# A seventh of w2 taken by a gather in mid-run instead of at the end: GQA decode attention beside a Mish layer, on one core

## The chip, the cores and the metric

One core of one Trainium2 chip. The metric is device time in microseconds of one launch, the median of several runs. Names of the engines: PE multiplies matrices (PEld is its weight load), DVE is the vector engine, ACT the scalar engine, POOL the general one, SP the one that issues most DMAs. Sixteen DMA engines move the bytes.

## What is computed

For 8 sequences, one new token each (D = 512), the result is the sum of three terms: the input, an attention block, and a two-layer block, both of the normalised input.

```python
xn = layernorm(x)                                   # x is 8 x 1 x 512
q  = xn @ wq                                        # 32 heads of 128
s  = q . k_cache * 128**-0.5                        # k_cache, v_cache: 8 x 8 x 8192 x 128
o  = softmax(s) . v_cache                           # four query heads share a KV head
A  = o @ wo                                         # wo is 4096 x 512
h  = xn @ w1 + b1                                   # w1 is 512 x 1792
act = h * tanh(softplus(h))                         # Mish
Bm = act @ w2                                       # w2 is 1792 x 512
out = x + A + Bm
```

All is float32. The two caches are 537 MB of the 561 MB that are read.

## The kernel before, in words

The work is cut into 32 units j = 0 to 31, each a sequence b = j % 8 and a pair of KV heads m = j // 8. A unit reads 8 MB of keys and 8 MB of values, each by one DMA of 128 partitions x 64 KB that SP issues (`load_unit`, L119). All of these land in one large tile `kv`. Its first quarter holds V (`V_AT`). The keys of even units lie at `ROW`, those of odd units half a place later at `ROW + ROW // 2`, so that two key loads overlap by half: the load of the next keys can be issued when the first half of the present scores is done.

The order of instructions is written out by hand; each engine runs its own in the order of the code, and waits are put in where data or places demand it. A unit goes: first half of `scores(j)` on PE (L284), issue of the keys of unit j+1, second half of `scores(j)`, `softmax(j)` (L294: DVE finds the maxima, PE turns them, ACT takes the exponentials), `values(j-1)` on PE (L346), issue of the values of unit j, `key_weights(j+1)` on DVE (L267), then `turn(j)`: PE brings the exponentials into another order by four products with `perm` (L323), a product with `ones` (L324), DVE transposes (L328) and sums (L334), and `merge(j-1)`. In unit 0 there is no `values`, and `mish` stands between `key_weights(1)` and `turn(0)`.

The start, before the loop: load of wq's first quarter into the tile `ws`, load of the keys of unit 0, small constant tiles on POOL and DVE, the layer norm, `xres` (the input in the layout of the result, L204), `selections` (L209), load of w1, `project(0)` (L223 to L242), load of the keys of unit 1, `spread` (L249).

`mish` (L367) multiplies by w1 and b1 on PE (L371, L380), computes the activation on DVE and ACT (L388 to L403) in a stretch of `kv` that begins at `W1_AT = ROW`, then lays it out by two products (L407), transposes it in blocks of 32 (L413) and copies what is needed to `aT` (L414). The keys of unit 2 later land on that same stretch. For the heads of the next quarter, `load_q` reads wq into `ws` in units 4, 12 and 20, and `project` uses it in units 5, 13 and 21.

The end: behind the loop SP issues four loads of wo (2 MB each) and three of w2 (2, 1 and 0.5 MB). PE does `values(31)`, the four steps of `outputs` with wo (L423), `merge`, and the products with w2 (`down`, L435), where a partition holds seven rows of 4 KB of w2. ACT copies wo's sum (L505); it is added to w2's sum by PE (L508) after the first w2 part. DVE adds `xres` (L518), and the result goes out (L519).

Of the kernel before, what the change touches and what calls it, by code (L numbers as in the profile page):

```python
# [20 lines left out]
F = 1792  # L21
# [3 lines left out]
G = 4  # L25
NH = 2
TG = SK // (NH * G) // P
BW = 1024
CC = D // P
FG = F // G  # L30
FT = 4
FP = FG // FT
Q = P // G
# [28 lines left out]
LOAD_Q, MAKE_Q, SPREAD_Q = 4, 5, 7  # L62


@with_exitstack
def kernel(
# [20 lines left out]
    kv = const.tile([P, PLACES], F32, name="kv")  # L87
    ws = const.tile([P, CC * BW], F32, name="ws")
# [4 lines left out]
    M = psum.tile([P, 512], F32, name="m")  # L93
    H = psum.tile([P, 512], F32, name="h")
# [15 lines left out]
    aT = const.tile([P, 2 * W2R, B], F32, name="aT")  # L110
    pt8 = const.tile([P, HALF, PL * TL, H2], F32, name="pt8")
    tr = const.tile([P, PL * TL, 32], F32, name="tr")

    def load_q(m):

        rows = wq.rearrange("j p f -> (j p f)").rearrange("(m p f) -> m p f", m=NP, p=P)
        nc.sync.dma_start(ws, rows[m])

    def load_unit(src, j, at):  # L119
        m, b = divmod(j, B)  # L120
        lo = (b * HKV + 2 * m) * NH * G
        t = kv[:, at : at + ROW]
        nc.sync.dma_start(
            t,
            src[lo : lo + NB].rearrange("j p f -> (j p f)").rearrange("(p f) -> p f", p=P),
        )
        return t


    low = kv[:B, W1_AT : W1_AT + 3 * D]  # L130
# [4 lines left out]
    for r in range(4):  # L135
        n = FG // 8
# [59 lines left out]
    for g in range(G):  # L196
# [170 lines left out]
    def mish(w1_t, b1_sb, flat):  # L367
        hp = H[:, :FG]
        for c in range(CC):
            for g in range(G):  # L370
                nc.tensor.matmul(  # L371
                    hp[Q * g : Q * g + B, :],
                    xnT[:, c, :],
                    w1_t[:, c * 2 + g // 2, g % 2 * FG : (g % 2 + 1) * FG],
                    start=(c == 0),
                    stop=False,
                )
        for g in range(G):
# [24 lines left out]
        nc.vector.tensor_mul(t1, t2, z)  # L403
        act = one
        half = FG // 2
        for e in range(2):
            nc.vector.tensor_mul(  # L407
                act.rearrange("p (i a e l) -> p e a l i", a=2, e=2, i=W2R)[:, e],
                h[:, half * e : half * (e + 1)].rearrange("p (a l i) -> p a l i", a=2, i=W2R),
                t1[:, half * e : half * (e + 1)].rearrange("p (a l i) -> p a l i", a=2, i=W2R),  # L410
            )
        turned = flat[:, 5 * FG : 6 * FG]
        nc.vector.transpose(turned, act)  # L413
        nc.vector.tensor_copy(aT, turned.rearrange("p (j q) -> p j q", q=Q)[:, :, :B])  # L414


    A = X[:, 0]

    def outputs(m, t):
        w = t.rearrange("p (u f) -> p u f", u=4)  # L420
        for d in range(2):
            for h in range(REP):
# [5 lines left out]
                    stop=(m == NP - 1 and d == 1),  # L428
                )

    def down(lo, hi, w):
        for j in range(2 * lo, 2 * hi):
            for g in range(G):
                at = (j - 2 * lo) * D + g * P
                nc.tensor.matmul(  # L435
                    H[Q * g : Q * g + B, :P],
                    aT[:, j, :],
                    w[:, at : at + P],
                    start=(j == 0),
                    stop=(j == 2 * W2R - 1),  # L440
                )


# [7 lines left out]
    for j in range(UNITS):  # L451
        b = j % B
        more = j // B + 1 < NP

        k = k_t.pop(j)
        scores(j, k, j % 2 == 1, 0)
        if j == UNITS - 1:
            v_t[j] = load_unit(v, j, K_AT[0])
        elif j > 0:
            k_t[j + 1] = load_unit(kT, j + 1, K_AT[(j + 1) % 2])  # L460
        scores(j, k, j % 2 == 0, 1)
        WK.pop(j)
        lsel = softmax(j)
        os = None
        if j > 0:
            os = values(j - 1, v_t.pop(j - 1))
        if j + 1 < UNITS:
            v_t[j] = load_unit(v, j, V_AT)
            if more and b == SPREAD_Q:
                spread(qT)  # L470
            key_weights(j + 1)
        if j == 0:
            mish(w1_t, b1_sb, kv[:, W1_AT : W1_AT + 6 * FG])
        if more and b == LOAD_Q:
            load_q(j // B + 1)
        if more and b == MAKE_Q:
# [9 lines left out]
    for m in range(NP):  # L486
# [4 lines left out]
    w2_rows = w2.rearrange("j p f -> (j p) f").rearrange("(q i) f -> q (i f)", i=W2R)  # L491
    w2_t = []
    parts = ((0, 4), (4, 6), (6, 7))
    for lo, hi in parts:
        t = kv[:, W2_AT + lo * BW : W2_AT + hi * BW]
        nc.sync.dma_start(t, w2_rows[:, lo * BW : hi * BW])  # L496
        w2_t.append(t)

    os = values(UNITS - 1, v_t.pop(UNITS - 1))
# [3 lines left out]
    outputs(NP - 1, w_o[NP - 1])  # L503
    a_sb = work.tile([P, 512], F32, name="e")
    nc.scalar.copy(a_sb, A)  # L505
    down(*parts[0], w2_t[0])
    for g in range(G):
        nc.tensor.matmul(  # L508
            H[Q * g : Q * g + B, :P],
            bsel[:, :B],  # L510
            a_sb[:, g * P : (g + 1) * P],
            start=False,
            stop=False,
        )
# [43 lines left out]
```

## Time and profile before

| | |
|---|---|
| median of 3 runs | 1313.15 us (1312.73 to 1313.54) |
| the profiled execution's own time | 1312.88 us |
| its span, first to last instruction | 1311.1 us |
| granted TensorE clock, mean | 0.872 |
| PE busy | 995.4 us (76%) |
| DVE busy | 515.6 us (39%) |
| ACT, POOL busy | 40.2 us, 4.4 us |
| DMA | 561.79 MB, 428 GB/s over the span |

The page cuts the span in 40 slices and gives each engine's share; it also follows back the chain of work that ended last. A row of a timeline reads: start in us, duration in us, engine, line, operation, out<-in, shapes, how many, and in brackets the engine's idle time before it and what ended that. A `q` behind an engine's name (SPq) means its instruction queue; a DMA row there is the issue, not the transfer. A row of busy times in a stretch reads: from:to, length, then busy time and count of PE, PEld, DVE, ACT and POOL (those that were asked for), granted clock, DMA share and GB/s. A float32 product shows as two matmuls on PE, so four products are eight.

### The profile page before, as it was taken

How to read it: one execution, taken by the hardware profiler on the slowest of the kernel's cores; microseconds unless marked ns; L12 is line 12 of the kernel's file. 1: busy time of each engine (PE TensorE's matmuls, PEld its weight loads, DVE VectorE, ACT ScalarE, POOL GpSimd, SP SyncE). 2: the span in 40 equal slices, each digit the busy share in tenths (PEclk: the TensorE clock that was granted, in tenths of full speed). 3: DMA queues.
4: the chain of work that ended last, by engine and by line, in shares of the span. 5: the costliest groups of instructions: out<-in, count | busy, mean ns of one | idle time of the engine just before them, and what ended most of it. 6: DMA issues, size and time to landing. Idle time of an engine off the chain costs nothing.

```text
span 1311.1 us, 11174 instructions
## 1 busy us (share of the span) xinstructions
PE 995.4 (76%) x5048; PEld 341.6 (26%) x5048; DVE 515.6 (39%) x728; ACT 40.2 (3%) x88; POOL 4.4 (0%) x13
## 2 busy tenths in 40 slices
PE   5978777778868768887878768687796678677766
PEld 3322222223322222232322222232232222222222
DVE  2373344432444442345342444413544433344431
ACT  1000000000000000000000000000000000000000
POOL 1000000000000000000000000000000000000000
PEclk9988878898887899778987888888888899787898
DMA  9999999999999999999999999999999999999998
GB/s 393 450 420 440 428 436 428 431 440 428 437 428 436 428 439 424 443 424 438 426 435 438 423 440 422 442 426 434 436 431 434 432 432 432 430 431 432 425 415 326
DMA packets 13711, 561.79 MB, mean 428 GB/s; under 512 B 1368, under 2 KB 1496, under 8 KB 4704
## 3 DMA queue, kind: packets, MB, share of 16 engines
q1 hardware_dynamic: 13520, 561.06, 99.3%
q8 instruction: 39, 0.64, 0.2%
q10 hardware_dynamic: 16, 0.02, 0.0%
q14 instruction: 8, 0.07, 0.0%
q0 software_dynamic: 128, 0.01, 0.0%
HBM read 561.01 MB, written 0.07 MB: 428 GB/s over the span
## 4 chain that ended last, share of the span: by engine, by line
DMA 72%; PE 23%; DVE 2%; SPq 2%; issue 0%; ACT 0%; POOL 0%; POOLq 0%; DVEq 0%
DMA kv<-in_v 70%; PE o L346 20%; DMA kv<-in_w 2%; SPq L496 2%; PE s L284 1%; DVE pt L334 1%; PE x L249 1%; PE m L234 0%; PE h L223 0%; PE h L371 0%; DVE kv L402 0%; DVE tr L328 0%; DVE wk L267 0%; POOL kv L137 0%; DVE nm L296 0%
## 5 line engine op out<-in xcount | busy, mean ns | idle before, releaser
L284 PE MATMUL s<-kv,wk 128*64 128x512 f32 x2048 | 509.7, 661 | 171.2 <-DMA kv<-in_kT 168.6
L346 PE MATMUL o<-kv,pt 128*32 128x512 f32 x2048 | 267.9, 683 | 49.1 <-DMA kv<-in_v 39.6
L284 PEld LDWEIGHTS s<-kv,wk 128*64 128x64 f32 x2048 | 157.0, 153 | 498.5 <-issue 324.5
L334 DVE TENSOR_REDUCE pt<-tr 64x512 f32<-64x2048 f32 x64 | 241.3, 3770 | 1.6
L296 DVE TENSOR_REDUCE nm<-s 128x1 f32<-128x512 f32 x32 | 22.1, 692 | 368.7 <-PE s L284 368.7
L323 PE MATMUL x<-e,perm 128*128 128x512 f32 x256 | 130.8, 658 | 2.0 <-ACT qr L256 2.0
L346 PEld LDWEIGHTS o<-kv,pt 128*32 128x32 f32 x2048 | 69.3, 123 | 221.3 <-issue 169.5
L354 DVE TENSOR_SCALAR os<-o,isel 128x128 f32<-128x128 f32 x32 | 11.2, 351 | 268.5 <-PE o L346 268.5
L328 DVE STREAM_TRANSPOSE tr<-x 128x512 f32<-128x512 f32 x128 | 78.7, 672 | 0.0
L323 PEld LDWEIGHTS x<-e,perm 128*128 128x128 f32 x256 | 50.8, 209 | 76.9 <-issue 74.5
L267 DVE TENSOR_TENSOR wk<-qr,mask 128x512 f32<-128x512 f32 x64 | 63.0, 1026 | 19.8 <-ACT qr L256 19.8
L315 ACT ACTIVATE e<-s,nmx 128x512 f32<-128x512 f32 x32 | 22.0, 687 | 1097.9 <-DVE nmx L312 1097.9
L356 DVE SCALAR_TENSOR_TENSOR os<-o,isel,os 128x128 f32<-128x128 f32 x96 | 33.7, 351 | 3.4
L297 PE MATMUL m<-ident,nm 128*1 128x128 f32 x32 | 8.7, 273 | 30.1 <-DVE nm L296 30.1
L308 PE MATMUL m<-ident,nx 1*128 1x1 f32 x32 | 7.0, 219 | 24.2 <-DVE nx L304 24.2
L326 DVE RECIPROCAL rt<-m 128x8 f32<-128x8 f32 x32 | 6.6, 207 | 38.5 <-PE m L324 38.5
L249 PE MATMUL x<-qT,tr 128*128 128x64 f32 x128 | 19.3, 315 | 3.0 <-ACT qr L256 2.7
L249 PEld LDWEIGHTS x<-qT,tr 128*128 128x128 f32 x128 | 18.1, 226 | 6.2 <-ACT qr L256 3.3
L363 PE MATMUL m<-hsel,os 128*128 128x8 f32 x64 | 12.4, 266 | 9.3 <-DVE rt L326 9.3
L317 DVE TENSOR_SCALAR lsel<-rsel,l 128x8 f32<-128x8 f32 x32 | 7.4, 231 | 30.1 <-ACT e L315 30.1
L297 PEld LDWEIGHTS m<-ident,nm 128*1 128x1 f32 x32 | 2.5, 79 | 58.3 <-DVE nm L296 58.3
L324 PEld LDWEIGHTS m<-lsel,ones 128*128 128x128 f32 x64 | 12.2, 190 | 15.8 <-issue 15.5
(89 smaller groups left out, 165.3 us busy)
## 6 DMA issues: line engine op xcount, KB each, us to landing
ws<-in_wq SPq DMA_DIRECT2D x4, 2048.0 KB, 34.3
kv<-in_wo SPq DMA_DIRECT2D x4, 2048.0 KB, 25.8
kv<-in_w SPq DMA_DIRECT2D x1, 3584.0 KB, 22.7
kv<-in_w SPq DMA_DIRECT2D x1, 2048.0 KB, 37.1
kv<-in_w SPq DMA_DIRECT2D x1, 1024.0 KB, 20.7
kv<-in_kT SPq DMA_DIRECT2D x32, 29.9
kv<-in_v SPq DMA_DIRECT2D x32, 29.9
kv<-in_w SPq DMA_DIRECT2D x1, 512.0 KB, 20.7
```

Of the source, the lines that this page charges most:

```text
L249: nc.tensor.matmul(X[:, half, k * 64 : (k + 1) * 64], wide[:, half * 8 + k], qT, start=True, stop=True,)
L267: nc.vector.tensor_mul(w[:, :, d], q[:, :, d].to_broadcast([P, DI, NH * G, REP]), mask[:, d * NH * G : (d + 1) * NH * G] .rearrange("p (o ...
L284: nc.tensor.matmul(S[64 * c : 64 * (c + 1), :], w[:, i].rearrange("p d k h -> p (d k h)"), kk[:, i, c, :], start=(part == 0 and n == 0), s ...
L296: nc.vector.tensor_reduce(nm, S, axis=AX.X, op=ALU.max, negate=True)
L315: nc.scalar.activation(e, S, AF.Exp, bias=nmx, accum_out=l)
L323: nc.tensor.matmul(X[:, g], perm[:, g], e, start=True, stop=True)
L328: nc.vector.transpose(tr.rearrange("p (l t) c -> p t l c", t=TL)[:, tl], X.rearrange("p g (t q l) -> p t l g q", t=TL, q=PP)[:, tl],)
L334: nc.vector.tensor_reduce(pt8[half, :, :, d * REP : (d + 1) * REP].rearrange("p c y h -> p y c h"), tr[half].rearrange("p y (g c h) -> p y ...
L346: nc.tensor.matmul(O[Q * q : Q * (q + 1), :], pt8[:, c, TL * l : TL * (l + 1), :].rearrange("p t h -> p (t h)"), vt[:, 512 * n : 512 * (n ...
L356: nc.vector.scalar_tensor_tensor(os, O[:, DH * i : DH * (i + 1)], isel[:, i : i + 1], os, op0=ALU.mult, op1=ALU.add)
L363: nc.tensor.matmul(M[:, 168 : 168 + H2], os, hsel, start=True, stop=True)
L496: nc.sync.dma_start(t, w2_rows[:, lo * BW : hi * BW])
```

## The change

A partition keeps six instead of seven rows of 4 KB of w2 for the end (written as twelve half rows of 2 KB, `FU`). The remaining 128 rows, half a MB, are read in unit 14 by an indirect DMA from POOL into `ws`, on 64 of the 128 partitions, 8 KB each (`load_extra`), and multiplied in unit 17 (`extra`), whose result is added to `xres`. Which partition takes which row stands in `RUNS`; the indices are built in the start by `find_rows` (POOL writes them as a row, DVE picks each partition's own). A second index tile, from `MARKS`, drives a gather of 36 rows of 256 B of wq in unit 26, whose data nobody reads. In `mish` the layout of the activation changes, the part that belongs to the gathered rows is put into `ex` by 20 small copies, and PE turns it into `eT`. At the end w2 comes in five transfers (1 MB, 768, 512, 512 and 256 KB), and wo's sum is added ahead of all w2 products instead of after the first part.

```diff
-W2R = 7
+W2R = 6
+FU = 2 * W2R
+FE = 4
+NONE = 65536
+MARKS = tuple(
+    (p0, p0, n)
+    for p0, n in ((0, 1), (4, 2), (8, 3), (16, 4), (28, 4), (60, 1), (64, 4), (96, 2))
+    + ((68, 4), (100, 3), (92, 4), (124, 4))
+)
+RUNS = (
+    ((0, 12), (16, 4)),
+    ((28, 4), (32, 12)),
+    ((48, 4), (60, 4), (64, 8)),
+    ((92, 4), (96, 8), (124, 4)),
+)
...
+LOAD_E, USE_E = 14, 17
...
+    def find_rows(idx, runs, flat):
+        table = flat[:, :P].bitcast(mybir.dt.int32)
+        real, mine = flat[:, P : 2 * P], flat[:, 2 * P : 2 * P + 1]
+        nc.gpsimd.memset(table, NONE)
+        for at, p0, n in runs:
+            nc.gpsimd.iota(table[:, p0 : p0 + n], pattern=[[1, n]], base=at, channel_multiplier=0)
+        nc.vector.tensor_copy(real, table)
+        nc.vector.tensor_mul(real, real, ident)
+        nc.vector.reduce_sum(mine, real, axis=AX.X)
+        nc.vector.tensor_copy(idx, mine)
...
     nc.vector.tensor_copy(xres, M[:, 256:384])
+    runs = []
+    for g in range(G):
+        at = FG // 4 * g + Q * W2R // 2
+        for p0, n in RUNS[g]:
+            runs.append((at, p0, n))
+            at += n
+    find_rows(idx, runs, kv[:, W1_AT + 7424 : W1_AT + 7424 + 2 * P + 1])
+    find_rows(idm, MARKS, kv[:, W1_AT + 7808 : W1_AT + 7808 + 2 * P + 1])
...
         act = one
-        half = FG // 2
-        for e in range(2):
-            nc.vector.tensor_mul(
-                act.rearrange("p (i a e l) -> p e a l i", a=2, e=2, i=W2R)[:, e],
-                h[:, half * e : half * (e + 1)].rearrange("p (a l i) -> p a l i", a=2, i=W2R),
-                t1[:, half * e : half * (e + 1)].rearrange("p (a l i) -> p a l i", a=2, i=W2R),
-            )
-        turned = flat[:, 5 * FG : 6 * FG]
-        nc.vector.transpose(turned, act)
+        nc.vector.tensor_mul(
+            act.rearrange("p (c e f) -> p e c f", c=2, e=2),
+            h.rearrange("p (e c f) -> p e c f", c=2, e=2),
+            t1.rearrange("p (e c f) -> p e c f", c=2, e=2),
+        )
+        rows = act.rearrange("p (c r) -> p c r", c=2)
+        mixed = flat[:, 5 * FG : 5 * FG + FU * Q]
+        turned = flat[:, 6 * FG : 6 * FG + FU * Q]
+        ex = flat[:, 7 * FG :].rearrange("p (t q) -> p t q", t=FE)
+        for c in range(2):
+            nc.vector.tensor_copy(
+                mixed.rearrange("p (i c l) -> p c l i", i=W2R, c=2)[:, c],
+                rows[:, c, : Q * W2R].rearrange("p (l i) -> p l i", i=W2R),
+            )
+        nc.vector.transpose(turned, mixed)
         nc.vector.tensor_copy(aT, turned.rearrange("p (j q) -> p j q", q=Q)[:, :, :B])
+        nc.vector.memset(ex, 0.0)
+        for g in range(G):
+            at = Q * W2R
+            for p0, n in RUNS[g]:
+                for c in range(2):
+                    nc.vector.tensor_copy(
+                        ex[Q * g : Q * (g + 1), c::2, p0 : p0 + n],
+                        rows[Q * g : Q * (g + 1), c, at : at + 2 * n].rearrange(
+                            "p (s i) -> p i s", i=2
+                        ),
+                    )
+                at += 2 * n
+        for t in range(FE):
+            nc.tensor.matmul(
+                M[:, 384 + t * B : 384 + (t + 1) * B], ex[:, t, :], bsel[:, :B], start=True, stop=True
+            )
+        nc.vector.tensor_copy(eT.rearrange("p t b -> p (t b)"), M[:, 384 : 384 + FE * B])
...
+    def load_extra():
+        nc.gpsimd.indirect_dma_start(
+            ws[:, : FE * D],
+            None,
+            w2.rearrange("j p f -> (j p f)").rearrange("(r f) -> r f", f=FE * D),
+            bass.IndirectOffsetOnAxis(ap=idx, axis=0),
+            bounds_check=F // FE - 1,
+            oob_is_err=False,
+        )
+
+    def extra():
+        for t in range(FE):
+            nc.tensor.matmul(
+                H[Q * t : Q * t + B, :], eT[:, t, :], ws[:, t * D : (t + 1) * D], start=True, stop=True,
+            )
+        part = work.tile([P, 512], F32, name="e")
+        nc.scalar.copy(part, H)
+        for g in range(G):
+            nc.tensor.matmul(
+                M[Q * g : Q * g + B, 256:384], bsel[:, :B], part[:, g * P : (g + 1) * P], start=True, stop=True,
+            )
+        nc.vector.tensor_add(xres, xres, M[:, 256:384])
...
+        if j == 26:
+            nc.gpsimd.indirect_dma_start(
+                ws[:, :64],
...
+        if j == LOAD_E:
+            load_extra()
+        if j == USE_E:
+            extra()
         if more and b == MAKE_Q:
             qT = project(j // B + 1)
         turn(j, lsel)
...
-    parts = ((0, 4), (4, 6), (6, 7))
+    parts = ((0, 4), (4, 7), (7, 9), (9, 11), (11, 12))
     for lo, hi in parts:
-        t = kv[:, W2_AT + lo * BW : W2_AT + hi * BW]
-        nc.sync.dma_start(t, w2_rows[:, lo * BW : hi * BW])
+        t = kv[:, W2_AT + lo * D : W2_AT + hi * D]
+        nc.sync.dma_start(t, w2_rows[:, :, lo * D : hi * D])
...
     nc.scalar.copy(a_sb, A)
-    down(*parts[0], w2_t[0])
     for g in range(G):
         nc.tensor.matmul(
             H[Q * g : Q * g + B, :P],
             bsel[:, :B],
             a_sb[:, g * P : (g + 1) * P],
-            start=False,
+            start=True,
             stop=False,
         )
-    for p, t in zip(parts[1:], w2_t[1:]):
+    for p, t in zip(parts, w2_t):
         down(*p, t)
```

More of the change, by code (lines that the diff above doesn't have):

```diff
@@ L109 @@
     oT = const.tile([P, NP, H2, B], F32, name="oT")
-    aT = const.tile([P, 2 * W2R, B], F32, name="aT")
+    aT = const.tile([P, FU, B], F32, name="aT")
+    eT = const.tile([P, FE, B], F32, name="eT")
+    idm = const.tile([P, 1], mybir.dt.uint32, name="idm")
+    idx = const.tile([P, 1], mybir.dt.uint32, name="idx")
     pt8 = const.tile([P, HALF, PL * TL, H2], F32, name="pt8")
@@ L429, in outputs @@
                 )
+    def load_extra():
[10 more added lines that the diff above has]
+            nc.tensor.matmul(
+                H[Q * t : Q * t + B, :],
+                eT[:, t, :],
+                ws[:, t * D : (t + 1) * D],
+                start=True,
+                stop=True,
+            )
[3 more added lines that the diff above has]
+            nc.tensor.matmul(
+                M[Q * g : Q * g + B, 256:384],
+                bsel[:, :B],
+                part[:, g * P : (g + 1) * P],
+                start=True,
+                stop=True,
+            )
+        nc.vector.tensor_add(xres, xres, M[:, 256:384])
     def down(lo, hi, w):
-        for j in range(2 * lo, 2 * hi):
+        for j in range(lo, hi):
             for g in range(G):
-                at = (j - 2 * lo) * D + g * P
+                at = (j - lo) * D + g * P
                 nc.tensor.matmul(
@@ L438, in down @@
                     w[:, at : at + P],
-                    start=(j == 0),
-                    stop=(j == 2 * W2R - 1),
+                    start=False,
+                    stop=(j == FU - 1),
                 )
@@ L472 @@
         if j == 0:
-            mish(w1_t, b1_sb, kv[:, W1_AT : W1_AT + 6 * FG])
+            mish(w1_t, b1_sb, kv[:, W1_AT : W1_AT + 7 * FG + FE * P])
         if more and b == LOAD_Q:
             load_q(j // B + 1)
+        if j == 26:
+            nc.gpsimd.indirect_dma_start(
+                ws[:, :64],
+                None,
+                wq.rearrange("j p f -> (j p f)").rearrange("(r f) -> r f", f=64),
+                bass.IndirectOffsetOnAxis(ap=idm, axis=0),
+                bounds_check=NONE // 2 - 1,
+                oob_is_err=False,
+            )
[3 more added lines that the diff above has]
+            extra()
         if more and b == MAKE_Q:
@@ L490 @@
         )
-    w2_rows = w2.rearrange("j p f -> (j p) f").rearrange("(q i) f -> q (i f)", i=W2R)
+    w2_rows = w2.rearrange("j p f -> (j p f)").rearrange("(g r) -> g r", g=G)
+    w2_rows = w2_rows[:, : Q * FU * D].rearrange("g (l f) -> g l f", l=Q)
     w2_t = []
-    parts = ((0, 4), (4, 6), (6, 7))
+    parts = ((0, 4), (4, 7), (7, 9), (9, 11), (11, 12))
     for lo, hi in parts:
-        t = kv[:, W2_AT + lo * BW : W2_AT + hi * BW]
-        nc.sync.dma_start(t, w2_rows[:, lo * BW : hi * BW])
+        t = kv[:, W2_AT + lo * D : W2_AT + hi * D]
+        nc.sync.dma_start(t, w2_rows[:, :, lo * D : hi * D])
         w2_t.append(t)
@@ L511 @@
             a_sb[:, g * P : (g + 1) * P],
-            start=False,
+            start=True,
             stop=False,
         )
-    for p, t in zip(parts[1:], w2_t[1:]):
+    for p, t in zip(parts, w2_t):
         down(*p, t)
```

## The prediction

> **What bounds the kernel now.** I read the page first (busy shares, then the chain), then the waits of the DMA queue, then the start and the end in order of time.
>
> ```profile
> span 1311.1 us, 11174 instructions
> DMA  9999999999999999999999999999999999999998
> DMA 72%; PE 23%; DVE 2%; SPq 2%; issue 0%; ACT 0%; POOL 0%; POOLq 0%; DVEq 0%
> SPq L123 <- PE s L284: 299.6, 31, 22.7
> SPq L123 <- DVE aT L414: 17.6, 1, 17.6
> ```
>
> The DMA line is over nine tenths in 39 of 40 slices, and the chain is DMA for 72%. So the kernel is a stream of bytes, and bytes that only change places cost what they cost before. Two things can move the time: a stretch in which the DMA engines have nothing queued, and the tail behind the last byte. SP issues a K or V load when its place is free, so the slack of each issue is what matters. The last two rows are SP's waits: 31 times a K load waits for PE's score matmuls, and once for `aT` (L414), in the start, where this change adds work. These are the rows of that stretch.
>
> ```profile
> 50.67 0.33 SPq L123 DMA_DIRECT2D kv<-in_v  x1
> 68.85 0.33 SPq L123 DMA_DIRECT2D kv<-in_kT  x1
> ```
>
> ```profile
> 56.61 3.70 PE L323 MATMUL x<-e,perm 128*128 128x512 f32 x8
> 60.37 13.95 PE L284 MATMUL s<-kv,wk 128*64 128x512 f32 x64
> ```
>
> ```profile
> 66.23 0.62 DVE L403 TENSOR_TENSOR kv<-kv 128x448 f32<-128x448 f32 x1
> 66.89 0.96 DVE L407 TENSOR_TENSOR kv<-kv 128x224 f32<-128x224 f32 x2
> 67.88 0.65 DVE L413 STREAM_TRANSPOSE kv<-kv 128x448 f32<-128x448 f32 x1
> 68.56 0.22 DVE L414 COPY aT<-kv 128x112 f32<-128x112 f32 x1
> ```
>
> V of unit 0 is issued at 50.67, K of unit 2 at 68.85 (I call them V0 and K2). PE passes from mish straight to turn(0) at 56.61 and to scores(1) at 60.37, while DVE works on mish until 68.78. K2's place holds mish's scratch and half of K1's, so its issue needs both the end of mish and the first half of scores(1) (half of 13.95, done near 67.4). Today mish ends last. Two DMA answers show how much room K2 has.
>
> ```profile
> DMA packets 24, 0.79 MB, mean 605 GB/s; under 512 B 12, under 2 KB 12, under 8 KB 12
> DMA to landing us min/median/max: 26.0/26.0/26.0
> DMA  0000000000000000000000000000000000024799
> ```
>
> The first is of 73.9 to 75.2 us: the 12 packets under 512 B are the marks with which 12 of the 16 engines close V0, and the other 12 are 64 KB rows of K2 that start at once. The second is V0's own landing: 50.67 + 26.0 = 76.67, so the last engines are done near 76.2. The third is of 1308.0 to 1309.5, in 40 slices: the output's transfer, issued at 1308.48 (row below) into empty engines, has its first packets in slice 35, at 1309.3. An issue needs some 0.85 us to its first packet. K2 at 68.85 is thus 74.8 - 0.85 - 68.85 = 5.1 us early for most engines, 6.5 for the last.
>
> **The change part by part.** (a) *mish gets a PE step in its middle.* After the activation DVE makes one product instead of two halves, two copies, the transpose of 384 columns, the copy to `aT`, a memset of 512 columns and 20 small copies into `ex`; then PE multiplies `ex` four times by `bsel`, and DVE copies the result to `eT`. Everything stands inside mish, in front of turn(0). PE takes its instructions in the order of the code, so turn(0), scores(1) and all behind them wait for the last small copy. That is the wait which the change adds, and queued behind it are turn(0) and scores(1) on PE, the transposes and sums of turn(0) on DVE (they wait for PE), and K2 on SP. The prices:
>
> ```profile
> 1.47 0.48 DVE L149 MEMSET o<- 128x512 f32 x1
> 4.66 0.99 DVE L155 COPY perm<-ident 128x16 f32<-128x16 f32 x8 [2.17 <-POOL perm L146]
> 14.44 1.89 DVE L209 COPY tr<-ident 128x2048 f32<-128x2048 f32 x1
> 16.70 1.88 PE L234 MATMUL m<-bsel,e 128*128 128x8 f32 x8 [0.70 <-ACT e L231]
> 244.64 5.18 PE L323 MATMUL x<-e,perm 128*128 128x512 f32 x8
> 562.59 6.63 PE L323 MATMUL x<-e,perm 128*128 128x512 f32 x8
> 1201.07 16.79 PE L284 MATMUL s<-kv,wk 128*64 128x512 f32 x64 [6.14 <-DMA kv<-in_kT]
> 1211.04 0.33 SPq L123 DMA_DIRECT2D kv<-in_kT  x1
> ```
>
> DVE from 66.89: product 0.62 (as L403); two copies of 192 columns, each L414's 0.22 plus 80 columns at 1.89/2048, 0.29, so 0.58; transpose 0.65 x 384/448 = 0.56; `aT` 0.22; memset 0.48; 20 copies at 0.99/8 = 0.12, 2.4. Sum 4.9: `ex` is ready at 71.8. The small copies are the uncertain part: at L414's 0.22 they are 4.4 and `ex` comes at 73.8; if they run together a little, 71.4.
>
> PE then does the four products: L234 does just such four (eight passes) in 1.88, so 73.7. Turn(0) took 3.70 at 56.61; it took 5.18 and 6.63 where PE came out of a stretch with little work. Here PE has been idle since 56.6, for 15 us, so I take 5.2 and keep 3.70 and 6.63 as ends: scores(1) starts at 73.7 + 5.2 + 0.06 = 79.0. Its first half is 7.0, or 1211.04 - 1201.07 = 9.97 after a wait; I take 7.0, since turn(0) has gone before. K2 is issued at 86.0 instead of 68.85.
>
> The granted clock shows what the 5.2 stands for:
>
> ```profile
> 561.70:568.50 6.80, 6.80 (x13) 3.39 (x13) 0.22 (x1) 0.00 (x0) 0.00 (x0) 0.50 0.91 388
> ```
>
> In this window, which holds nearly all of the 6.63 us turn, PE ran at 0.50 for 6.8 us though it was busy throughout. The Trainium skill ("TensorE: Matmul & The Clock Gate", "Part 1: The HAM clock gate") says that PE falls to half clock after an idle window of about 3.4 us and is released after about 3.4 us of sustained work. By that rule only 1.5 us of turn(0) would run slow, it would take about 4.5, and the sum below would be 0.7 smaller (an estimate from the Trainium skill's figure); the trace shows a slow stretch twice as long.
>
> The first bytes of K2 then come at 86.0 + 0.85 = 86.9. Twelve engines were empty around 74.8, the others by 76.2: idle for 12.1 and 10.7 us. I take **12.0**, since most engines have the long gap. Ends: all fast, 71.4 + 1.0 (the four products at half of what they cost there; an estimate) + 3.70 + 0.06 + 7.0 = 83.2, idle 7.9 on the last engines; all slow, 73.8 + 1.9 + 6.63 + 0.06 + 9.97 = 92.4, idle 18.4. No later stage gives this back, as the DMA line has no slack elsewhere.
>
> What is late next: scores(1) ends at 79.0 + 13.95 = 93.0, DVE has turn(0)'s transposes and sums done by then (79.0 + 2.46 + 7.55, rows below). In unit 30 the next V is issued 1229.25 - 1217.86 = 11.4 us after the scores' end (1201.07 + 16.79), so V1 comes at 104.4, first bytes 105.3. K2 leaves the engines at 86.9 + 19.35 = 106.2 (one load is half of the 38.7 us between the two V issues below). That holds by 0.9 us; if PE stays slow, a gap of a microsecond or two more is possible here, and it lies within the ends. From there the rhythm is the old one.
>
> ```profile
> 68.81 2.46 DVE L328 STREAM_TRANSPOSE tr<-x 128x512 f32<-128x512 f32 x4
> 71.37 7.55 DVE L334 TENSOR_REDUCE pt<-tr 64x512 f32<-64x2048 f32 x2
> 1190.55 0.33 SPq L123 DMA_DIRECT2D kv<-in_v  x1
> 1229.25 20.24 SPq L123 DMA_DIRECT2D kv<-in_v  x2
> ```
>
> (b) *Building the indices* (24 POOL instructions, 8 on DVE, before the selections). POOL is free at 5.5 (first row below). DVE, which starts the selections at 14.44 now, first does its eight, 1.8 at L414's 0.22, then the selections' 1.89: done at 18.1. The spread that reads them can't start before qT, 23.02 + 0.23. Cover 5.1 us: zero. If that cover goes, each microsecond counts fully (second rival).
>
> ```profile
> 4.57 0.94 POOL L147 MEMSET pt<- 128x1024 f32 x1
> 23.02 0.23 DVE L242 TENSOR_SCALAR qT<-m 128x64 f32<-128x64 f32 x1 [6.69 <-PE m L234]
> 728.69 1.12 PE L284 MATMUL s<-kv,wk 128*64 128x512 f32 x2 [4.90 <-DMA kv<-in_kT]
> ```
>
> (c) *The gather in unit 14 and extra() in unit 17.* Queued on POOL, which has nothing else then; it waits for the projection's reads of `ws` in unit 13. extra() adds on PE eight passes of 512 columns (3.57/16 each by L423 below, 1.8), ACT's copy (0.58 by L505) and eight passes like L508 (0.40): 2.9 us with the joints, ahead of turn(17). PE then waits 4.90 us for K18 anyway (third row above), so it is hidden. SP's next load of `ws` is three units later. The index gather of unit 26 moves 36 rows of 256 B into a tile that nobody reads: zero.
>
> (d) *The end.* SP issues five transfers where it issued three, 3 MB for 3.5 MB.
>
> ```profile
> 1266.66 21.33 SPq L496 DMA_DIRECT2D kv<-in_w  x3
> 1298.98 3.57 PE L423 MATMUL x<-kv,oT 128*8 128x512 f32 x16 [2.98 <-DMA kv<-in_wo]
> 1302.67 0.58 ACT L505 COPY e<-x 128x512 f32<-128x512 f32 x1 [43.58 <-PE x L423]
> 1303.77 1.93 PE L435 MATMUL h<-kv,aT 128*8 128x128 f32 x64 [1.22 <-DMA kv<-in_w]
> 1305.52 0.40 PE L508 MATMUL h<-e,bsel 128*8 128x128 f32 x8
> 1307.47 0.62 PE L435 MATMUL h<-kv,aT 128*8 128x128 f32 x16 [0.17 <-DMA kv<-in_w]
> 1302.60:1304.60 2.00, 0.83 (x32) 0.83 (x36) 0.00 (x0) 0.58 (x1) 0.00 (x0) 1.00 0.58 242
> 1308.48 0.35 SPq L519 DMA_DIRECT2D out<-os  x1
> ```
>
> SP has its last w2 issue out at 1288.0; two more, even at 5 us each, are out well before the output at 1308.48: zero. In the old time frame PE gets wo's sum at 1303.25, adds it in 0.40, and has 48 products of w2 left (96 passes at 1.93/64 = 0.03, 2.9, and 0.2 for the joints): 1306.8, where it ended at 1308.1. The row of 1302.60 says why this may hold: in those 2 us the DMA share is 0.58, so some seven of 16 engines are already done, and the others set the end. If the gathered half MB rides on engines that are ahead, the lagging ones lose 32 KB each, 1.2 us at 512 KB in 19.35, and the tail gains 1.3. If it rides on all 16, the old bytes are only earlier, and 0.3 is left from the shorter last transfer. If it rides on the lagging ones, 64 KB more and 32 KB less, it costs 1.1. No row tells which; I take **-0.8**, nearer to the first, between it and the second.
>
> The Trainium skill ("DMA: Bandwidth & Descriptors", "The descriptor swizzle") gives each engine fixed groups of four partitions; by it the 64 partitions chosen belong to just eight engines, eight rows each. Whether these are the ones that are ahead it doesn't say; if they are, the tail term is -1.3.
>
> **Sum.** 12.0 - 0.8 = +11.2 us on the profiled execution's 1312.88 (span 1311.1): 1324.1. The median shown is 1313.15, so this is +0.8%; a change of 0.2%, 2.6 us, is about what a measurement of this kernel can tell from none.
>
> **The rivals.** *No gap, no change.* PE would have to run turn(0) and scores(1) ahead of the four products. Then scores(1) ends at 74.3 as now, the products at 76.2, and K2 is issued between 74 and 76.2: idle 0 to 2.3, less 0.8, **1313**. It decides from K2's issue before 74.0. For it: PE does run ahead of DVE at 56.61. Against it: only because nothing in front of turn(0) waits there; every row of PE stands in the code's order.
>
> *POOL holds the start.* DVE's work after POOL's last is 0.9 and the selections 1.89, so POOL must end by 20.5; if it needs over 0.62 us for each of 24 instructions, the selections, the spread and all of unit 0 move. At 0.94, its longest compute row, it ends at 28.1, 7.6 late: **1332**. Against it: the memset behind that row writes 1024 columns, these one to 128. The Trainium skill ("GPSIMD Engine Reference", "2.1 Instruction dispatch") adds some 6 us for the first call of a function freshly loaded; by that the limit falls to 0.37 each. No row here shows such a call.
>
> *The gather lands on lagging engines*, +1.1 in place of -0.8: **1326**. It doesn't hide the gap, it adds to it.
>
> **How the numbers follow.** Forecast 0.83, no gap 0.08, POOL 0.05, gather 0.04. Predicted 1324.1. The ends of all sums are 1312.88 + 7.9 - 1.3 = 1319.5 and 1312.88 + 18.4 + 1.1 = 1332.4; the upper needs every price at its worst, so the range is 1319 to 1330, which leaves out the no-gap case, the POOL case and a rest. Forecast, POOL and gather are slower, 0.92, of which I keep 0.02 back for a gap that PE or SP shortens in a way I don't see: slower 0.90. The other 0.10 is the no-gap case: same 0.07 and, with the best tail, faster 0.03.
>
> **What would show it.** Right: K2 issued near 86 instead of 68.85, PE idle some 15 us between L380 and the four products, one slice of the DMA line far below nine early on, V issues 38.7 apart from there, all later marks 11 to 13 us late, and a tail from wo's last landing to the end about 1 us shorter. Wrong: K2 issued before 75; or POOL still busy past 20 us; or a second gap ahead of V1; or the gather's unit longer than its neighbours by more than the 1.2 us of its bytes.

## The result, and the profile after

The changed kernel takes 1345.72 us (1344.48 to 1347.57, 4 runs) against 1313.35 us before: ratio 1.0248, 95% interval 1.0231 to 1.0266, or 32 us. I had forecast 1324.1 with a range to 1330. The profiled execution took 1344.48 us, 31.6 more than that of before. One execution of `before_step` (below) took 3280.78 us and fell in a slow state, so it is left out. Two lines of the page:

```profile
span 1342.5 us, 11256 instructions
DMA  9969999999999999999999999999999999999992
```

The DMA line shows two holes. The third slice has fallen from nine tenths to six: that is the gap at the start which I forecast. The last slice has fallen from eight to two: that one I did not forecast. First the start, by SP's waits and by the instructions of PE, DVE and SP in order of time:

```profile
SPq L141 <- DVE kv L464: 20.2, 1, 20.2
```

```profile
68.72 1.91 DVE L464 COPY kv<-kv 32x24 f32<-32x24 f32 x20
70.61 1.87 PE L472 MATMUL m<-bsel,kv 128*128 128x8 f32 x8 [14.64 <-DVE kv L464]
72.33 5.24 PE L361 MATMUL x<-e,perm 128*128 128x512 f32 x8
77.63 13.95 PE L322 MATMUL s<-kv,wk 128*64 128x512 f32 x64
84.80 0.33 SPq L141 DMA_DIRECT2D kv<-in_kT  x1
100.68 0.33 SPq L141 DMA_DIRECT2D kv<-in_v  x1
```

PE sits idle for 14.64 us until the last of the 20 small copies, then does the four products, turn(0) at a low pace, and scores(1). SP's wait of 20.2 us for the copies (L464) ends with them at 70.63; then K2 waits 14 us more, for the first half of scores(1), and is issued at 84.80 instead of 68.85. How much of the stream this cost is read from the moments at which PE starts on keys or values that it has waited for. First the keys of unit 5, then the keys and values of unit 14 and the keys of unit 15 (the gather runs beside these); before, then after:

```profile
212.71 16.05 PE L284 MATMUL s<-kv,wk 128*64 128x512 f32 x64 [6.32 <-DMA kv<-in_kT]
...
573.30 16.65 PE L284 MATMUL s<-kv,wk 128*64 128x512 f32 x64 [3.28 <-DMA kv<-in_kT]
592.65 8.63 PE L346 MATMUL o<-kv,pt 128*32 128x512 f32 x64 [0.66 <-DMA kv<-in_v]
612.04 16.06 PE L284 MATMUL s<-kv,wk 128*64 128x512 f32 x64 [6.32 <-DMA kv<-in_kT]
...
1293.78 1.90 PE L423 MATMUL x<-kv,oT 128*8 128x512 f32 x16 [0.55 <-DMA kv<-in_wo]
```

```profile
224.52 16.20 PE L322 MATMUL s<-kv,wk 128*64 128x512 f32 x64 [6.15 <-DMA kv<-in_kT]
...
584.90 16.92 PE L322 MATMUL s<-kv,wk 128*64 128x512 f32 x64 [4.69 <-DMA kv<-in_kT]
605.79 9.82 PE L384 MATMUL o<-kv,pt 128*32 128x512 f32 x64 [1.94 <-DMA kv<-in_v]
625.16 15.14 PE L322 MATMUL s<-kv,wk 128*64 128x512 f32 x62 [5.09 <-DMA kv<-in_kT]
...
1306.47 1.90 PE L484 MATMUL x<-kv,oT 128*8 128x512 f32 x16 [0.82 <-DMA kv<-in_wo]
1313.86 3.60 PE L484 MATMUL x<-kv,oT 128*8 128x512 f32 x16 [5.17 <-DMA kv<-in_wo]
1319.00 1.06 PE L527 MATMUL h<-kv,aT 128*8 128x128 f32 x32 [0.40 <-DMA kv<-in_w]
1326.44 1.47 PE L527 MATMUL h<-kv,aT 128*8 128x128 f32 x24 [6.38 <-DMA kv<-in_w]
1331.43 1.04 PE L527 MATMUL h<-kv,aT 128*8 128x128 f32 x16 [3.52 <-DMA kv<-in_w]
1336.61 1.04 PE L527 MATMUL h<-kv,aT 128*8 128x128 f32 x16 [4.14 <-DMA kv<-in_w]
1339.00 0.62 PE L527 MATMUL h<-kv,aT 128*8 128x128 f32 x8 [1.35 <-DMA kv<-in_w]
```

The difference is 11.8 us at unit 5 and 11.6 at unit 14: the gap at the start, and nothing more until there. Across the gather it becomes 13.1, and at the third step of wo it is 12.7 (1306.47 - 1293.78). From that step to the end of the span it took 17.3 us before (1311.1 - 1293.78) and takes 36.0 now: the missing 18.7 us all lie there. The last step of wo starts 7.4 us behind the third where it was 5.2, and then PE waits for one w2 transfer after the other, 6.38, 3.52, 4.14 and 1.35 us. What those transfers do meanwhile, in a stretch in which nothing but w2 moves (the last two columns are the DMA share and GB/s):

```profile
1319.00:1331.00 12.00, 2.53 (x56) 1.52 (x56) 0.00 (x0) 0.00 (x0) 0.00 (x0) 0.60 0.25 105
```

The DMA share is 0.25 with transfers queued. In the trace's records of single packets, four packets of w2 are under way during 93% of this stretch, and hardly ever fewer. So four of sixteen engines work, at 26 GB/s each. The new view of w2, `g (l f) -> g l f`, has the four groups of 448 features as its outermost dimension.

### The profile page after: what moved, and what is told of

Same layout as the page of the kernel before. It is cut to its first block, busy times and chain, and to the rows that moved or that the text cites. A ratio compares the mean times of both kernels' runs of the same rounds, so it can differ in the third digit from the quotient of the medians.

```text
span 1342.5 us, 11256 instructions
## 1 busy us (share of the span) xinstructions
PE 991.3 (74%) x5056; PEld 341.2 (25%) x5056; DVE 519.1 (39%) x760; ACT 40.8 (3%) x89; POOL 8.9 (1%) x39
## 4 chain that ended last, share of the span: by engine, by line
DMA 71%; PE 23%; SPq 3%; DVE 2%; issue 0%; ACT 0%; POOL 0%; POOLq 0%
DMA kv<-in_v 69%; PE o L384 19%; SPq L602 3%; PE s L322 2%; DMA kv<-in_w 2%; PE x L287 1%; PE x L361 0%; PE m L272 0%; PE h L261 0%; PE h L409 0%; DVE kv L440 0%; DVE wk L305 0%; POOL kv L167 0%; PE m L472 0%; DVE kv L464 0%
## 5 line engine op out<-in xcount | busy, mean ns | idle before, releaser
L384 PE MATMUL o<-kv,pt 128*32 128x512 f32 x2048 | 263.9, 674 | 54.1 <-DMA kv<-in_v 44.5
L527 PE MATMUL h<-kv,aT 128*8 128x128 f32 x96 | 5.2, 365 | 15.8 <-DMA kv<-in_w 15.8
```

The source lines that it names most:

```text
L384: nc.tensor.matmul(O[Q * q : Q * (q + 1), :], pt8[:, c, TL * l : TL * (l + 1), :].rearrange("p t h -> p (t h)"), vt[:, 512 * n : 512 * (n ...
```

## The experiments

Two theories stood at the outset for the end: that the view with 4 outermost leaves w2 on four engines (V), or that the order, the number or the sizes of the five transfers are at fault (P). For the start: that the wait of PE and K2 for the products is the whole 12 us (S), or that something else in the early part is.

**The view at the end.** `end16` cuts each transfer into four of 32 partitions:

```diff
-        nc.sync.dma_start(t, w2_rows[:, :, lo * D : hi * D])
+        for g in range(0, G, 1):
+            nc.sync.dma_start(t[Q * g : Q * (g + 1)], w2_rows[g, :, lo * D : hi * D])
```

> The changed kernel with one edit: each of the five w2 transfers is issued as four, one for each group of 32 partitions; pieces, pitch and places stay. Theory A (four engines: the view of w2 has an outermost dimension of 4, and the transfer runs on four of 16 DMA engines): w2's last landing comes about 7 to 8 us behind wo's last instead of 25, DMA share there well over 0.22, and the time falls by 19 to 20 us to about 1326. Theory B (the small pieces at a pitch of 24 KB are slow in themselves): the time stays within 2 us of 1345.7.

Measured: 1332.55 us, ratio 1.0149 (1.0132 to 1.0166); 13 us of the expected 20 came back. In the end of `end16` the DMA share is no longer a quarter:

```profile
1303.00:1327.00 24.00, 14.55 (x166) 4.93 (x158) 1.58 (x5) 0.59 (x1) 0.00 (x0) 0.72 0.81 220
```

So the view mattered, but either it was not all or the cut had a price. `uniform` keeps whole transfers and lets a partition keep the first six of its seven old rows, so that the view has 128 outermost. The seventh rows then lie elsewhere in w2, and two gathers of 4 KB a partition bring them instead of one of 8 KB. The lines that change the view:

```diff
-    w2_rows = w2.rearrange("j p f -> (j p f)").rearrange("(g r) -> g r", g=G)
-    w2_rows = w2_rows[:, : Q * FU * D].rearrange("g (l f) -> g l f", l=Q)
+    w2_rows = w2.rearrange("j p f -> (j p) f").rearrange("(q i) f -> q (i f)", i=W2R + 1)
...
-        nc.sync.dma_start(t, w2_rows[:, :, lo * D : hi * D])
+        nc.sync.dma_start(t, w2_rows[:, lo * D : hi * D])
```

> The changed kernel, but the six rows a partition keeps for the end are the first six of its seven (one pitch for all 128 partitions, so the view of w2 has 128 outermost instead of 4), still five transfers of the same sizes; the seventh rows come by two gathers of 4 KB instead of one of 8 KB, onto the same 64 partitions. Theory V (the view with 4 outermost confines each w2 transfer to four of the sixteen engines, and that is the whole 18.8 us that I missed at the end; cutting the transfers into pieces of 32 partitions gave back only 13 because the pieces have a cost of their own): DMA share at the end near 1.0 and w2's last landing about 5 to 6 us behind wo's last one minus overlap, as before; the time falls by 20 to 1325 (1323 to 1327), my original sum. Rival P (w2 at the end is slow for another reason: five transfers, the gaps between the rows, or the many issues): the time stays at 1332 or above, as with the cut transfers.

Measured: **1325.03 us** (1324.81 to 1326.24), ratio 1.0094 (1.0078 to 1.0109): 20.7 less than the changed kernel, with the same five transfers in the same order. PE in the end of `uniform`:

```profile
1312.58 2.74 PE L488 MATMUL x<-kv,oT 128*8 128x512 f32 x16 [2.46 <-DMA kv<-in_wo]
1316.04 0.61 PE L617 MATMUL h<-e,bsel 128*8 128x128 f32 x8 [0.73 <-ACT e L615]
1316.43 2.39 PE L532 MATMUL h<-kv,aT 128*8 128x128 f32 x72
1319.31 1.04 PE L532 MATMUL h<-kv,aT 128*8 128x128 f32 x24 [0.50 <-DMA kv<-in_w]
```

The waits of 6.38, 3.52 and 4.14 us are gone; 72 of 96 passes run through, and only 0.50 us is waited for w2. Theory P falls. `before4` turns it round: the kernel before, with nothing but a view of four groups for w2. It moves as many bytes in the same three transfers, but some rows of w2 are left out and others read in their place, so its result is not that of the layer.

```diff
-    w2_rows = w2.rearrange("j p f -> (j p) f").rearrange("(q i) f -> q (i f)", i=W2R)
+    w2_rows = w2.rearrange("j p f -> (j p f)").rearrange("(g r) -> g r", g=G)
+    w2_rows = w2_rows[:, : Q * 6 * BW].rearrange("g (l f) -> g l f", l=Q)
...
-        nc.sync.dma_start(t, w2_rows[:, lo * BW : hi * BW])
+        nc.sync.dma_start(t, w2_rows[:, :, min(lo, 5) * BW : min(hi, 6) * BW])
```

> The kernel before, where only the view of w2 at the end is changed: grouped by four outermost with another pitch inside the group (so wrong rows are read, and the third transfer reads the sixth row again; the same three transfers, the same 3.5 MB, 128 partitions each). No gather, nothing moved. Theory V: w2 runs on four engines; 3.5 MB cost 18.8 x 3.5/3 = 22 more: 1335 (1330 to 1339), DMA share 0.25 in the last 20 us. Rival P (five transfers or their order made the end slow): no change, 1313.

Measured: 1346.46 us (1341.26 to 1347.95), ratio 1.0244 (1.0224 to 1.0264): 33 us from the view alone, where I had expected 22. The size was a miss, and this row of `before4` holds most of it:

```profile
1304.00:1324.00 20.00, 2.30 (x12) 0.17 (x4) 0.00 (x0) 0.59 (x1) 0.00 (x0) 0.50 0.25 85
```

The share is again 0.25, but at 85 GB/s instead of 105. The first transfer has rows of 16 KB. By the trace's packet records, 60 of its 128 packets took under 0.7 us, as all 128 do in the kernel before (0.62 on the mean, on sixteen engines), but 45 took 1.1 us or more; the mean is 0.88. Over four engines this makes 128 x 0.26 / 4, some 8 of the 11 us that I missed (an estimate from these means). So the size of the row alone is not what slows them; what does was not tried. `end2` asks whether it is the outermost size that caps the engines:

```diff
+        for g in range(0, G, 2):
+            nc.sync.dma_start(t[Q * g : Q * (g + 2)], w2_rows[g : g + 2, :, lo * D : hi * D])
```

> The changed kernel, but each of the five w2 transfers is two of 64 partitions, so the view has 2 outermost. Theory V (the outermost size caps the engines of one transfer): two engines for each transfer. If both take the same two, 3 MB at 2 x 26 = 52 GB/s is 58 us where four engines took 29: 1375 (1368 to 1380), share 0.13. If they take different ones, as now: 1346. Rival (the cap is not the outermost size but the 32 partitions of a group, or the number of transfers): 64-partition pieces on more engines, 1335 or below.

Measured: 1373.09 us (2 runs), ratio 1.0458 (1.0439 to 1.0477). In its end, with ten transfers of 64 partitions:

```profile
1330.00:1365.00 35.00, 3.55 (x56) 1.77 (x56) 0.00 (x0) 0.00 (x0) 0.00 (x0) 0.50 0.13 52
```

The share is 0.13 and the rate 52 GB/s: two engines, and both halves use the same two. Halves on engines of their own would run side by side, since a transfer does not wait for the whole of the one ahead: 6 KB packets of the second pair start at 1324.2, while 8 KB packets of the first pair run until 1325.3. Nor is it the number of transfers: ten are slower than five here, and the twenty of `end16` were faster. The Trainium skill ("DMA: Bandwidth & Descriptors", "Rules for kernel authors") states it: "an outermost dim of size c < 16 ... confines the whole DMA to at most c engines"; the traces agree, 0.25 for four and 0.13 for two.

What the cut of `end16` cost is shown by `best_cut`, which cuts the transfers of `best` (below) in the same way:

```diff
-        nc.sync.dma_start(t, w2_rows[:, lo * D : hi * D])
+        for g in range(G):
+            nc.sync.dma_start(t[Q * g : Q * (g + 1)], w2_rows[Q * g : Q * (g + 1), lo * D : hi * D])
```

> The kernel 'best' (one pitch for w2's rows, products in unit 3), but each w2 transfer at the end is cut into four of 32 partitions (20 issues instead of 5). Theory X (pieces of 32 partitions are slow by themselves, which is why cutting gave back only 13 of 20 us at the four-group view): + 7.5 us over 'best', 1321.6 (1319 to 1324), 8 KB packets at 0.45 us and above while they move. Rival (the cut pieces were slow only because of the other pitch of that view): no change, 1314.

Measured: 1322.19 us, 8.1 over `best`, so the cut has a price by itself, as expected. The stretch in which they move, in `best_cut`, and its like in `best`:

```profile
1292.00:1309.00 17.00, 11.05 (x102) 3.07 (x98) 1.57 (x5) 0.58 (x1) 0.00 (x0) 0.79 0.87 243
```

```profile
1292.00:1305.00 13.00, 9.85 (x110) 2.99 (x106) 1.57 (x5) 0.58 (x1) 0.00 (x0) 0.87 0.88 354
```

The engines are just as busy, 0.87 and 0.88, but move 243 instead of 354 GB/s: sixteen engines writing to the same 32 partitions take longer for the same bytes. Both stretches hold some of wo's rows too, but w2's own packets show the same: an 8 KB packet took 0.48 us on the mean instead of 0.32, a 6 KB one 0.37 instead of 0.24. That they get in each other's way at those partitions is my reading; only the price is shown. Nor is it separated how much of the 8.1 us comes from the twenty issues, the last of which SP has out only at 1310.7.

**The start.** `before_step` is the kernel before with the memset, the 20 copies, the four products and the copy to `eT` put into mish, and nothing else of the change:

```diff
         nc.vector.tensor_copy(aT, turned.rearrange("p (j q) -> p j q", q=Q)[:, :, :B])
+        nc.vector.memset(ex, 0.0)
...
+        for t in range(FE):
+            nc.tensor.matmul(
+                M[:, 384 + t * B : 384 + (t + 1) * B], ex[:, t, :], bsel[:, :B], start=True, stop=True
+            )
+        nc.vector.tensor_copy(eT.rearrange("p t b -> p (t b)"), M[:, 384 : 384 + FE * B])
```

> The kernel before with the one step alone: the memset, the 20 small copies into ex, the four products on PE and the copy to eT inside mish; nothing reads eT. Theory S: K2 is issued near 86 instead of 68.85 and the time rises by 11 to 13 us to about 1325. Theory S2: it rises by at most 3 us.

Measured: 1325.09 us (three runs, 1324.88 to 1326.45), ratio 1.0095 (1.0075 to 1.0115), 11.9 over the 1313.20 of before on the same chip. The empty stretch in `before_step`:

```profile
74.00:85.00 11.00, 11.00 (x43) 4.14 (x43) 6.90 (x7) 0.00 (x0) 0.00 (x0) 0.91 0.01 1
```

For 11 us PE is busy throughout, and the DMA share is 0.01. Theory S is shown. `start` undoes the step in the changed kernel: `ex` goes into `ws`, and the products come in unit 1.

```diff
-        ex = flat[:, 7 * FG :].rearrange("p (t q) -> p t q", t=FE)
+        ex = ws[:, : FE * P].rearrange("p (t q) -> p t q", t=FE)
...
         turn(j, lsel)
+        if j == 1:
+            turn_extra()
```

> The changed kernel with one edit: ex lies in ws instead of on the place of K2, and its four products and the copy to eT come behind turn(1) instead of inside mish; DVE's copies stay where they are. Theory S (the order: PE waits in front of turn(0), K2 is issued late and the DMA engines stand empty): K2 is issued at 70 to 71, no gap, the time falls by 11 to 13 us to about 1333.5. Theory S2 (the longer mish on DVE and the index building cost the time, or a later stage gives the gap back): the time stays within 3 us of 1345.7.

Measured: 1336.82 us, ratio 1.0181 (1.0164 to 1.0198), 9 of the expected 12. A second wait had come with my placement, as `start` shows:

```profile
96.51 1.06 PE L475 MATMUL m<-bsel,ws 128*128 128x8 f32 x8 [0.30 <-DVE rt L364]
106.70 0.60 PE L401 MATMUL m<-hsel,os 128*128 128x8 f32 x2 [9.13 <-DVE eT L478]
107.22 15.82 PE L322 MATMUL s<-kv,wk 128*64 128x512 f32 x64
```

```profile
111.00:117.00 6.00, 6.00 (x30) 1.97 (x28) 0.00 (x0) 0.00 (x0) 0.00 (x0) 1.00 0.44 186
```

DVE's copy to `eT` stands behind its sums of turn(1); `merge` writes to the same PSUM tile and so waits 9.13 us for it, and scores(2) and the keys of unit 3 (K3) queue behind `merge`. From 111 to 117 us the DMA share is 0.44, where the kernel before has 0.99: a second gap. It is the same kind of mistake as the change's own, one unit later. `start3` puts the products ahead of a turn, in unit 3:

```diff
+        if j == 3:
+            turn_extra()
         turn(j, lsel)
```

> The changed kernel, but ex lies in ws and the four products with the copy to eT come in unit 3, ahead of turn(3), instead of inside mish. Theory S (the start costs 12.5 us because turn(0), scores(1) and K2 wait behind the products, and the second gap of the first try was made by my placement behind turn(1)): K2 is issued near 71, K3 without a gap, and the time falls by 12.5 to 1333 (1331.5 to 1334.5). Rival: the second gap belongs to the late K2 or to the 20 copies themselves, and the time stays near 1337.

Measured: 1334.06 us, ratio 1.0161 (1.0146 to 1.0177), 11.7 less than the changed kernel. SP in the start of `start3`:

```profile
70.53 0.33 SPq L141 DMA_DIRECT2D kv<-in_kT  x1
92.73 0.33 SPq L141 DMA_DIRECT2D kv<-in_v  x1
104.16 0.33 SPq L141 DMA_DIRECT2D kv<-in_kT  x1
```

K2 goes out at 70.53, and K3 at 104.16, where `start` had it at 116.22: neither gap is left, and the 20 copies, which are still in mish, cost nothing.

**Both repaired.** `both` joins `end16` and `start`.

> Both edits (w2 in transfers of 32 partitions, ex in ws with its products behind turn(1)). Theories A and S: the two losses are separate and add up, and what is left is the prediction's tail term: 1312 to 1313.5, no measurable difference from before. If a third loss is hidden (the gather, extra, 20 issues on SP): 1315 or more.

Measured: 1325.04 us, ratio 1.0091 (1.0075 to 1.0108), where 1312 to 1313.5 was expected. Nearly 12 us over before are left. The price of the pieces (7.5 us, `end16` less `uniform`) and the second gap (2.8, `start` less `start3`) are 10.3 of them; the next kernel, without either, is 1.1 over before. `best` joins `uniform` and `start3`.

> Both edits: one pitch for w2's rows at the end, and the products in unit 3. If V and S are the whole difference, only the gather itself and the order of the tail are left of the change: my tail term, -0.8, so 1312.5 (1311.5 to 1313.5). If the gather's half MB rides on engines that are not ahead, +1.1: 1314.5. If something of the change that I have not found costs more, 1317 or above.

Measured: **1314.13 us** (1312.80 to 1314.71, 11 runs) against 1313.01 for before (15 runs): ratio 1.0010 (1.0001 to 1.0019). That is outside the 1311.5 to 1313.5 which my tail term gave, and near the 1314.5 for a gather on engines that are not ahead. So the two faults are the whole 32 us, to about one; and a seventh of w2 moved to mid-run, with nothing else in the way, gains nothing that can be measured.

**What the gather is worth.** Where its rows land and when it runs, `best_other` and `late` vary. `best_other` uses the other 64 partitions:

```diff
-    ((0, 12), (16, 4)),
-    ((28, 4), (32, 12)),
-    ((48, 4), (60, 4), (64, 8)),
-    ((92, 4), (96, 8), (124, 4)),
+    ((12, 4), (20, 8), (44, 4)),
+    ((52, 8), (72, 8)),
+    ((80, 12), (104, 4)),
+    ((108, 16),),
```

> The kernel 'best', but the gathered rows go to the other 64 partitions (RUNS is the complement; eight runs instead of ten, 16 small copies instead of 20). My tail term said: on engines that are ahead -1.3, on the lagging ones +1.1. If the choice of partitions matters so, 2.4 us above 'best': 1316.5. If the engines are equally busy in mid-run, so that the half MB costs its 1.2 us wherever it goes: as 'best', 1314.1 (1313.3 to 1315).

`late` issues it behind the loop, beside wo's loads, and uses it ahead of the last step of wo:

```diff
-        if j == LOAD_E:
-            load_extra()
-        if j == USE_E:
-            extra()
...
+    load_extra()
...
+    extra()
     outputs(NP - 1, w_o[NP - 1])
```

> The kernel 'best', but the two gathers are issued at the very end, beside wo's loads, into the last 2048 columns of kv (free once scores(31) is done), and extra() comes ahead of the last step of wo. The same bytes in all; nothing is moved to mid-run any more, only half a MB is taken at the end by the chosen 64 partitions. Theory (the gather in unit 14 pays the full 1.2 us of its bytes in mid-run, and the tail gains as much from having less to load): mid-run as before (V of unit 31 lands 1.0 earlier than in 'best'), and if the chosen engines are ahead at the end, nothing is lost there: 1312.9 (1312.0 to 1313.5). If they are not ahead, or the gather's small rows disturb wo's loads: 1314 to 1317.

Measured: 1314.33 us, ratio 1.0011 (1.0002 to 1.0020), and 1314.31 us, ratio 1.0009 (1.0000 to 1.0018). Neither differs from `best`. For `best_other` this rules out 1316.5, so by the time the choice of partitions does not matter. For `late` it is a miss: the theory gave 1312.0 to 1313.5, and the measured time lies in the rival's range. PE's starts around unit 14, in `best`, `best_other` and `late`:

```profile
573.33 15.95 PE L326 MATMUL s<-kv,wk 128*64 128x512 f32 x64 [6.70 <-DMA kv<-in_kT]
593.52 8.77 PE L388 MATMUL o<-kv,pt 128*32 128x512 f32 x64 [2.20 <-DMA kv<-in_v]
613.48 16.35 PE L326 MATMUL s<-kv,wk 128*64 128x512 f32 x64 [6.75 <-DMA kv<-in_kT]
```

```profile
574.00 16.27 PE L326 MATMUL s<-kv,wk 128*64 128x512 f32 x64 [3.81 <-DMA kv<-in_kT]
...
615.46 16.03 PE L326 MATMUL s<-kv,wk 128*64 128x512 f32 x64 [7.61 <-DMA kv<-in_kT]
```

```profile
573.47 16.76 PE L326 MATMUL s<-kv,wk 128*64 128x512 f32 x64 [4.96 <-DMA kv<-in_kT]
...
612.16 16.19 PE L326 MATMUL s<-kv,wk 128*64 128x512 f32 x64 [6.17 <-DMA kv<-in_kT]
```

From the keys of unit 14 to those of unit 15 it took 38.74 us before. It takes 40.15 in `best` (+1.4), 41.46 in `best_other` (+2.7) and 38.69 in `late` (none). The gather thus pays for its bytes where it runs, 1.2 us at the rate of a load. Whether the partition adds to that stays open: the nine profiled executions with the gather on the chosen partitions took 38.96 to 40.59, and the 41.46 is a single one. In the end the profiled `best` gets its bytes back:

```profile
1300.03 2.68 PE L491 MATMUL x<-kv,oT 128*8 128x512 f32 x16 [2.42 <-DMA kv<-in_wo]
...
1306.76 1.04 PE L535 MATMUL h<-kv,aT 128*8 128x128 f32 x24 [0.49 <-DMA kv<-in_w]
```

The last step of wo starts 1.05 us later than before (1300.03 for 1298.98), and the span ends 0.5 earlier (1310.6 for 1311.1). But the profiled execution of `best` (1312.80) is the fastest of its eleven, and that of `late` (1312.86) too. By the medians all three kernels are 1.1 to 1.3 over before, `late` as well, which has nothing of the gather in mid-run. What costs this microsecond is open.

## Why the prediction was wrong, by its own steps

**(a) The start: right.** Forecast 12.0 us of idle engines, measured 11.6 to 11.8 at units 5 and 14, 11.9 in the time of `before_step` and 11.7 given back by `start3`. Its terms, forecast and measured: `ex` ready at 71.8 and 70.63 (the small copies took 0.10 each, not 0.12), the products 1.9 and 1.87, turn(0) 5.2 and 5.24, K2 issued at 86.0 and 84.80. The slow turn(0) decided for the row of 5.18 rather than the clean 3.70. V of unit 1 (V1) I had forecast at 104.4, with 0.9 us to spare; it was issued at 100.68, 3.7 earlier, so the stretch that I called tight was not.

**(b) The indices: right at zero.** POOL's 22 index writes took 0.86 and 1.03 us in all, over at 8.1 us, so the rival that POOL holds the start was far off (it needed 0.62 us each; these took 0.09).

```profile
5.97 0.86 POOL L153 IOTA kv<- 128x12 int32 x10
...
7.05 1.03 POOL L153 IOTA kv<- 128x1 int32 x12
```

**(c) extra(): hidden**, as forecast: it stands in unit 17, and the keys of unit 18 start 12.6 us later than before (741.25 for 728.69), no more than the 11.6 of the start and the 1.2 of the gather's bytes together. Those bytes I had booked as only moved, inside the tail term; in the profiled `best` that is right in sum.

**(d) The end: this step failed.** I priced 3 MB for 3.5 MB, two issues more on SP and the products left behind the last byte. The rule that I had set at the outset, that bytes which only change places cost what they cost before, put the new view of w2 at nothing: I took for granted that the new transfers run on all sixteen engines as the old ones did. The diff shows the view, and I read it only for the sizes of its pieces. The runs show the transfers on four engines (share 0.25, 105 GB/s), for 20.7 us between the changed kernel and `uniform`. The bytes fit this: at four times 26 GB/s, 3 MB need 30 us, and at the 428 GB/s of the whole run some 7 (an estimate from these rates); the rest of the difference of 23 I put down to what runs beside wo.

With that one view repaired the kernel takes 1325.03 us, and the forecast, 1324.1, stands 0.9 from it. So the mechanism of the start and its size were right, and the small distance owes something to luck, since the tail term in it was not borne out. SP's two further issues at zero were right in `uniform`, where all five are out by 1304.1:

```profile
1281.84 22.28 SPq L606 DMA_DIRECT2D kv<-in_w  x5
```

The range failed for the same reason: its upper end took every price of (a) at its worst, and no price at all for the view. The tail term itself, -0.8, is -0.5 in the profiled `best`, the fastest of its runs, and +1.1 by the medians. The rival of the lagging engines had +1.1 too, but it rests on the choice of partitions, which made no difference in the time of `best_other`, so that agreement is luck.

## What to carry to other kernels

When a diff rewrites the view of a transfer, read its outermost dimension before its bytes: a DMA share that stays at a clean fraction while transfers are queued (0.25 and 0.13 here) was the sign that they ran on that part of the engines. Transfers cut into pieces of 32 partitions kept the engines as busy here and still moved a third less, so the repair is a view with all 128 partitions outermost. And a product inside a stretch of another engine's work holds up all later work of PE, so it is put where PE and the copy behind it wait for nothing.

## What the runs showed of the hardware that was not expected

Transfers with outermost size 2 share the same two engines even when two of them are queued side by side (52 GB/s together). Packets of 16 KB on four engines took 0.88 us on the mean, from 0.61 to 1.27, where on sixteen engines in the kernel before none took more than 0.63. Pieces of 32 partitions held the engines 0.87 busy at 243 GB/s, where whole transfers moved 354 at 0.88; their 8 KB packets took 0.48 us instead of 0.32.
